# The last of 32 attention periods split into two of 256 queries, and three of four last output tiles finished from copied partial sums

## The chip, the cores and the metric

One NeuronCore of one Trainium2 chip runs the whole kernel. The metric is device time in microseconds (us) of one launch; lower is better. A separate profiled execution gives the trace.

## The reference, cut to what matters

Inputs are `x` (2048 tokens of 512 features), two sets of weights (A and B), and a gate vector. Branch A is full attention with 32 heads of width 16; branch B is a dilated local attention (8 keys per query, step 2); a gate mixes the two for each token.

```python
qkv = x @ wqkv                                   # A: H = 32, Dh = 16, S = 2048
scores = einsum("bhqd,bhkd->bhqk", q, k) * Dh ** -0.5
p = softmax(scores); a = (p @ v) @ wo            # per head, then one projection
b = local_attention(x)                           # 8 keys per query, own weights
out = g * a + (1 - g) * b                        # g = sigmoid((x * gate_w).sum(-1))
```

The exponentials of branch A are 32 heads of 2048 x 2048 numbers. They are most of the work.

## The kernel before, in words

**Periods and blocks.** Branch A is cut into 32 periods (L416): four chunks of 512 queries (`QW`, L32), and in each chunk eight groups of four heads. Within a period a *block* is one key tile of 128 keys for one head: 16 tiles times 4 heads is 64 blocks of 128 x 512 scores. The scores of a block are one matmul of 32 rows (the head's features padded to a strip) by 512 query columns; four heads sit in four row strips of the array and run beside each other. Probabilities times values is one matmul of 17 output rows (16 values and the softmax sum) into a column strip of an accumulator bank in PSUM (`pv_mm`, L1230).

**Two ways to an exponential.** Most blocks go to ScalarE (ACT): the scores of three or two blocks fill one of two PSUM rings (`rA` with three banks, `rB` with two), and one ACTIVATE makes the exponential of 1536 or 1024 columns (L1391 to L1406). The table `n_dve` (L20) says how many blocks of each period go to VectorE (DVE) instead, in groups of three (`d_set`, L1295): one operation per block turns scores into bit patterns (tile `dt_a` or `wkv`), three more per group add offsets to the three blocks at once (tile `pd_a`), and each of the four versions is multiplied with its own weighted values. A DVE group is thus six DVE operations and twelve value matmuls, and costs ScalarE nothing. From period `FLAT0` on (L34, L1341) the offset operation is written as one run of 1536 elements instead of six runs of 256. Before, the last four periods have 12, 15, 15 and 15 blocks on DVE.

**End of a period.** When a period's accumulator is complete, DVE transposes it (`po1`, L1428), takes the reciprocal of the sums, multiplies by reciprocal and gate (`po2`, `po2a`, `po2b`; on GpSimd except in the last two periods, L1432), and after every second period transposes the result into `oat` (`po3`, L1449). These are the inputs of the output projection.

**Output.** For each of 16 tiles of 128 tokens (loop at L1475), a PSUM bank collects four matmuls of branch B (`obt` times `bwo`) and four of branch A (`oat` times `woarr`); the bank is copied to SBUF and sent to DRAM by one transfer of 128 KB. For the last chunk the fourth `oat` matmul exists only after the last period. Before, its tiles are treated in two ways: tiles 2 and 3 have their first matmuls (nh = 3) evacuated early into unused memory (`fa_view`, L1471) and the last matmul goes to a ring bank, and DVE adds the two; tiles 0 and 1 keep their partial sums in two pinned PSUM banks, the last matmul adds to them, and ScalarE copies them out. So behind the last `po3` there are four matmuls, two DVE adds, two ScalarE copies and four transfers (three issued by SP, one by ScalarE).

**What sets the order.** All operations are put into one list with estimated durations, due times and dependences, and `list_schedule` (L180) writes out one fixed order for each engine; engines then run in that order. The planner also puts in filler matmuls of zeros (`zeros`, L1555) where it sees TensorE with too little to do. Three PSUM banks (`Banks(3)`, L407) are shared by accumulators, DVE scores, projections and fillers; two more rings take the scores for ScalarE.

Of the kernel before, what the change touches and what calls it, by code (L numbers as in the profile page):

```python
# [19 lines left out]
    n_dve=(3, 3, 6, 6, 9, 9, 12, 12) + (12,) * 21 + (15,) * 3,  # L20
# [13 lines left out]
FLAT0 = 29  # L34
# [89 lines left out]
SMD = 0.0  # L124
FIN, QB, KB, WO = 52.0, 0.0, 0.0, 26.0
# [181 lines left out]
def kernel(  # L307
# [108 lines left out]
    periods = [(c_, i) for c_ in range(NC) for i in range(NG)]  # L416
    NP = len(periods)
    n_dve = cfg["n_dve"]
# [3 lines left out]
    for pi in range(NP):  # L422
        first_unit.append(nu)
        n = n_dve[pi]
        assert n % NGR == 0 and n <= 4 * NTD
        taken = [(t, j) for t in vtiles for j in range(4)][:n]
        rest = [(t, j) for t in range(NT) for j in range(4) if (t, j) not in taken]
# [429 lines left out]
    def q_pair(pi, dl, rel):  # L857
# [35 lines left out]
        def get(e):  # L893
            def s():
                qt_tiles[pi + e] = work.tile([128, QW], BF16, name="qt", tag="qt", bufs=4)
                SP.dma_start(out=qt_tiles[pi + e][:], in_=_ap(q_scr[8 * (pi + e):8 * (pi + e) + 1, :], [[QW, 128], [1, QW]]))
            return s
# [10 lines left out]

    for pi in range(2, NP, 2):
        q_pair(pi, S0[pi] - QD, max(19.0, S0[pi - 2] - 2.0))  # L910


# [311 lines left out]
    for pi in range(NP):  # L1224
        for j in range(4):
            todo[(pi, j)] = NT + (NV - 1) * sum(1 for g in seq[pi][1] for x in g if x[1] == j)
# [3 lines left out]
    def pv_mm(pi, t, j, rhs, lhs):  # L1230
        c_, i = periods[pi]
        if pi not in acc_tiles:
            acc_tiles[pi] = misc_ps([128, QW], tag="acc")
# [14 lines left out]
    def pv_run(mine, tn):  # L1248
# [4 lines left out]
        def pv():  # L1253
            js = [j for j in range(4) if (pi, j) in first_pv and todo[(pi, j)] >= 1]
            j0 = st["op"].js[0]
            for _ in range(st["op"].filled):
                assert j0 in js
                mm(acc_tiles[pi][32 * j0:32 * j0 + 32, :], z32[:], z_bc, False, False, tile_position=(0, 32 * j0))
            for g_, s_, _, t, j in mine:
                pv_mm(pi, t, j, g_["p"][:, s_, :], vp_all[:, t])  # L1260
# [5 lines left out]
        o = op("pe", 0.0, pv, tn + 3.0, mode="c", js=js, full=-(-len(js) // 4), fill=not first,  # L1266
               deps=[g_["ex"] for g_ in gs] + [o_v[(4 * periods[pi][1] + j, t)] for _, _, _, t, j in mine]
# [27 lines left out]
    def d_set(pi, gi, t, j, qk_, tn):  # L1295
# [18 lines left out]
        def dq():  # L1314
            st["x"] = misc_ps([128, QW])
            mm(st["x"][:], kt_all[32 * j:32 * j + 32, i, t * 128:(t + 1) * 128], qt_tiles[pi][32 * j:32 * j + 32, :],
               True, True, tile_position=(32 * j, 0))
# [4 lines left out]
        deps = [o_q[pi], o_k[i][t // TPC], o_vd[(4 * i + j, t)]]  # L1322
# [10 lines left out]
        vs = [o_vd[(4 * i + j_, t_)] for t_, j_ in zip(g["ts"], g["js"])]  # L1333
# [14 lines left out]
        def pv(m, pb):  # L1348
            def s():
                for n1, (t_, j_) in enumerate(zip(g["ts"], g["js"])):  # L1350
                    pv_mm(pi, t_, j_, pb[:, n1, 0:QW], vd_all[:, m - 1, t_ - (NT - NTD)] if m else vp_all[:, t_])
# [30 lines left out]
    for k, us in enumerate(sets):  # L1382
# [18 lines left out]
        kd = [o_k[periods[pi][1]][t // TPC] for pi, t, j in us]  # L1401
# [17 lines left out]
    for pi, (c_, i) in enumerate(periods):  # L1419
# [3 lines left out]
        if i % 2 == 0:  # L1423
            ott_tok[pi // 2] = tok("ott", 1)
        ta, to = tok("accT", 1), ott_tok[pi // 2]
        E = S0[pi + 1]

        def po1(pi=pi, st=st):  # L1428
            st["a"] = work.tile([128, BPC, 32], FP32, name="accT", tag="accT", bufs=1)
            V.transpose(out=st["a"][:].rearrange("p b d -> p (b d)"), in_=acc_tiles[pi][:])  # L1430

        by_v = PO_V or pi >= NP - 2  # L1432
        E_ = V if by_v else G

        def po2(pi=pi, st=st):
            rden = work.tile([128, BPC], FP32, name="rden", tag="rden", bufs=2)
            V.reciprocal(out=rden[:], in_=st["a"][:, :, DH:DH + 1].rearrange("p b o -> p (b o)"))
            st["rd"] = rden

        def po2a(st=st, c_=c_, E_=E_):  # L1440
            E_.tensor_tensor(out=st["rd"][:], in0=st["rd"][:], in1=g_rw[:, c_ * BPC:(c_ + 1) * BPC], op=ALU.mult)

        def po2b(pi=pi, st=st, E_=E_):
            rden = st["rd"]
            rd_bc = _ap(rden[:], [list(rden[:].ap[0]), [1, BPC], [0, DH]])
            E_.tensor_tensor(out=ott2[:, 0, :, DH * (pi % 2):DH * (pi % 2 + 1)], in0=st["a"][:, :, 0:DH], in1=rd_bc,
                            op=ALU.mult)

        def po3(pi=pi, c_=c_, i=i):  # L1449
            if c_ not in oat_tiles:  # L1450
                oat_tiles[c_] = work.tile([128, NH, QW], BF16, name="oat", tag="oat", bufs=1)
            V.transpose(out=oat_tiles[c_][:, i // 2, :], in_=ott2[:, 0].rearrange("p b d -> p (b d)"))
        a = op("dve", 0.64, po1, E - PO1D, deps=o_pv[pi], alloc=[ta], use=[acc_tok[pi], acc_two[pi]])
        tr_ = tok("rden", 2)
        a = op("dve", 0.29, po2, E + 4.0, deps=[a], alloc=[tr_], use=[ta])
        al, us = [to] if i % 2 == 0 else [], [ta, tr_] + ([to] if i % 2 else [])
        if by_v:
            a = op("dve", 0.0, po2a, E + 4.0, deps=[a, o_gr], use=[tr_], parts=TT(BPC))
            a = op("dve", 0.0, po2b, E + 4.0, deps=[a], alloc=al, use=us, parts=TT(BPC * DH))
# [7 lines left out]
        prev = [o_oat[pi - 2]] if pi > 1 else []  # L1467
        o_oat[pi] = op("dve", 0.64, po3, E + 6.0, deps=[a, half] + prev, alloc=[oat_tok[c_]] if i == 1 else [],
                       use=[to] + ([oat_tok[c_]] if i > 1 else []))

    def fa_view(tt):  # L1471
        flat = kt_all[:, 0:NG - 1, :].rearrange("p g s -> p (g s)")
        return flat[:, tt * 2 * QW:(tt + 1) * 2 * QW].bitcast(FP32)

    for t in range(NT):  # L1475
# [3 lines left out]
        ng = NG - 2 if last else NG  # L1479
        nh = ng // 2  # L1480
        E = S0[NG * c_ + ng]
        dl = E + (4.0 + 4.0 * tt if last else 2.0 + 4.0 * tt)
        pin = last and tt < 2
        if pin:
            dl = S0[NP] - 1.0
# [13 lines left out]
        def ab_ev(st=st, tt=tt, last=last):  # L1499
            if last:  # L1500
# [6 lines left out]
        def dout(st=st, t=t):  # L1507
            SP.dma_start(out=out2d[t * 128:(t + 1) * 128, :], in_=st["o"][:, 0:D])
        tk = tok("misc", 2)
        a = None  # L1510
        for k0 in range(0, DC + nh, 2):
            nk = min(2, DC + nh - k0)
            a = op("pe", WAVE(nk), ab_part(k0), dl - 2.0 + 0.3 * k0, full=nk,
                   deps=[a] if k0 else [o_oat[NG * c_ + ng - 1], o_wo] + ([d_last[0]] + o_pv[NP - 1][:len(o_pv[NP - 1]) - (8, 0)[tt]] if pin else []) + o_obt[t:t + 1],
# [5 lines left out]
        elif pin:  # L1520
            tos = tok("osb", 2)

            def tail(st=st, c_=c_, tt=tt):
                mm_ct(st["pf"], oat_tiles[c_][:, NH - 1, tt * 128:(tt + 1) * 128], woarr[:, NH - 1, :], False, True)

            def t_ev(st=st):
                st["o"] = work.tile([128, D], BF16, name="osb", tag="osb", bufs=2)
                A.copy(out=st["o"][:, 0:D], in_=st["pf"][:])
            b = op("pe", 0.26, tail, S0[NP] + 60 + tt, deps=[o_oat[NP - 1], a], use=[tk, oat_tok[c_]])
            b = op("act", 0.6, t_ev, S0[NP] + 3 + tt, deps=[b, a], alloc=[tos], use=[tk])  # L1530

            def dout_a(st=st, t=t):
                A.dma_start(out=out2d[t * 128:(t + 1) * 128, :], in_=st["o"][:, 0:D])
            op(("sp", "act")[tt], 0.6, (dout, dout_a)[tt], S0[NP] + 4 + tt, deps=[b], use=[tos], lat=2.2)
        else:
            a = op("dve", 0.61, ab_ev, dl, deps=[a], use=[tk])
            tag = ("rB", "rA")[tt - 2]
            otag = "kvs"
            tk, tos = tok(tag, 2 if tag == "misc" else 1), tok(otag, 2)
            E2 = S0[NP] - 2.0  # L1540

            def tail(st=st, c_=c_, tt=tt, tag=tag):
                st["pt"] = misc_ps([128, D], tag=tag)
                mm_ct(st["pt"], oat_tiles[c_][:, NH - 1, tt * 128:(tt + 1) * 128], woarr[:, NH - 1, :], True, True)

            def t_ev(st=st, t=t, otag=otag):
                st["o"] = work.tile([128, D if otag == "osb" else 2 * D], BF16, name="osb", tag=otag, bufs=2)
                V.tensor_tensor(out=st["o"][:, 0:D], in0=st["pt"][:], in1=st["fa"], op=ALU.add)
            b = op("pe", 0.26, tail, E2 + tt, deps=[o_oat[NP - 1], a], alloc=[tk], use=[oat_tok[c_]])
            b = op("dve", 0.61, t_ev, E2 + 1 + tt, deps=[b, a], alloc=[tos], use=[tk])  # L1550
            def dout_a(st=st, t=t):
                A.dma_start(out=out2d[t * 128:(t + 1) * 128, :], in_=st["o"][:, 0:D])
            op("sp", 0.6, dout, E2 + 2 + tt, deps=[b], use=[tos], lat=2.2)
# [46 lines left out]
```

## Time and profile before

| what | us |
|---|---|
| three runs of the kernel | 805.14, 806.64, 807.27 |
| median | 806.64 |
| the profiled execution's own time | 805.02 |
| its span in the trace | 803.2 |
| ScalarE busy, share of the span | 778.0, 97% |
| TensorE busy (pipelined, not a measure of peak) | 742.8, 92% |
| VectorE busy | 689.1, 86% |
| GpSimd busy | 634.5, 79% |

Times in the trace count from the start of the span. A row of the timeline gives the start, the length, the engine, and how many instructions of one kind were merged into it; a bracket at the end gives idle time before it and what ended that. PE is TensorE, PEld its weight loads, ACT ScalarE, DVE VectorE, POOL GpSimd; SPq and ACTq are instructions that issue transfers. L378 and L369 are helpers that record every matmul and every instruction of the other engines, so operations are told apart by their tiles, not by their line.

### The profile page before, as it was taken

What the parts mean: (1) busy time and instruction counts of PE and PEld (TensorE: products, weight loads), DVE (VectorE), ACT (ScalarE), POOL (GpSimd) and SP (SyncE); (2) the same over time, 40 slices, a digit from 0 to 9 for tenths busy, and PEclk for the clock granted to TensorE, in tenths of its full rate; (3) what the DMA queues carried; (4) which work ended last, traced back from release to release, by engine and by line L of the source; (5) the groups of instructions that cost most, each with busy time, mean ns of one, the idle gap of its engine ahead of it and who ended that gap; (6) DMA issues with size and microseconds to landing.
All of it is one profiled execution on the core that took longest, in us unless ns stands there. A gap on an engine that the chain in (4) does not pass through costs nothing.

```text
span 803.2 us, 17445 instructions
## 1 busy us (share of the span) xinstructions
PE 742.8 (92%) x6651; PEld 240.5 (30%) x6708; DVE 689.1 (86%) x1098; ACT 778.0 (97%) x701; POOL 634.5 (79%) x1067
## 2 busy tenths in 40 slices
PE   8989999999999999999999999999989999889997
PEld 5333333332222222222222222222222323223222
DVE  5638787998896999999998999898998899888786
ACT  3999999999999999999999999999999999999996
POOL 4196979998999997999989899999999999940000
PEclk9999999999999999999999999999999999999999
DMA  8503171716345525245444535343534442000000
GB/s 264 145 16 106 30 168 53 170 42 165 86 93 138 126 74 151 60 117 122 110 108 116 123 98 139 82 118 108 142 85 105 128 119 62 19 8 21 1 1 28
DMA packets 58886, 77.19 MB, mean 96 GB/s; under 512 B 3745, under 2 KB 50849, under 8 KB 58801
## 3 DMA queue, kind: packets, MB, share of 16 engines
q1 hardware_dynamic: 52608, 53.91, 21.8%
q0 software_dynamic: 6048, 22.02, 14.7%
q8 instruction: 52, 0.85, 0.5%
q14 instruction: 34, 0.27, 0.1%
q10 hardware_dynamic: 144, 0.13, 0.0%
HBM read 43.78 MB, written 10.26 MB: 67 GB/s over the span
## 4 chain that ended last, share of the span: by engine, by line
ACT 50%; PE 25%; issue 22%; DVE 2%; DMA 1%; SPq 0%; ACTq 0%
ACT pT L369 49%; PE misc_ps L378 17%; PE ring L378 8%; DMA xld<-in_A_x_dram 1%; ACT lg L369 1%; DVE pd_a L369 0%; DVE wkv L369 0%; DVE kt_all L369 0%; PE pxt L635 0%; DVE dt_a L369 0%; DVE vd_all L369 0%; DVE vp_all L369 0%; ACT xT L369 0%; SPq L369 0%; DVE ssum L369 0%
## 5 line engine op out<-in xcount | busy, mean ns | idle before, releaser
L369 ACT ACTIVATE pT<-ring 128x1536 bf16<-128x1536 f32 (+1 forms) x677 | 769.5, 1324 | 8.8 <-PE ring L378 5.2
L378 PE MATMUL ring<-qt,kt_all 32*128 32x512 bf16 x1691 | 266.8, 382 | 45.5 <-ACT pT L369 37.2
L378 PE MATMUL misc_ps<-pT,vp_all 128*17 128x512 bf16 (+1 forms) x1691 | 201.6, 384 | 0.3 <-DVE dt_a L369 0.2
L369 POOL TENSOR_TENSOR prod<-ksh,qb 128x256 f32<-128x256 bf16 x256 | 174.4, 752 | 27.4 <-DMA ksh<-kv_scr 24.5
L378 PEld LDWEIGHTS <-kt_all 32*128 32x128 bf16 x2048 | 90.6, 91 | 297.8 <-issue 288.9
L369 POOL TENSOR_TENSOR prod<-prod 128x256 f32<-128x256 f32 (+1 forms) x256 | 172.0, 687 | 5.9
L369 DVE TENSOR_SCALAR pd_a<-wkv 128x1536 uint16<-128x1536 uint16 x198 | 169.1, 882 | 2.2 <-PE misc_ps L378 1.7
L369 DVE TENSOR_SCALAR wkv<-misc_ps 128x512 uint16<-128x512 f32 x198 | 132.3, 682 | 27.2 <-PE misc_ps L378 25.6
L369 DVE TENSOR_SCALAR pd_a<-dt_a 128x1536 uint16<-128x1536 uint16 x159 | 140.3, 905 | 0.9
L378 PE MATMUL misc_ps<-pd_a,vd_all 128*17 128x512 bf16 x1071 | 133.9, 382 | 0.1
L378 PE MATMUL misc_ps<-z 128*32 128x512 bf16 x399 | 132.3, 388 | 1.6 <-DVE z L369 1.6
L378 PE MATMUL misc_ps<-qt,kt_all 32*128 32x512 bf16 x357 | 129.0, 381 | 2.0 <-DVE wkv L369 0.5
L369 DVE TENSOR_SCALAR dt_a<-misc_ps 128x512 uint16<-128x512 f32 x159 | 106.6, 683 | 28.2 <-PE misc_ps L378 25.0
L369 POOL TENSOR_TENSOR prod<-vsh,lg 128x256 f32<-128x256 bf16 x128 | 82.7, 760 | 0.0
L378 PEld LDWEIGHTS <-vp_all 128*17 128x17 bf16 (+1 forms) x2048 | 54.3, 88 | 85.3 <-issue 72.5
L369 POOL TENSOR_TENSOR av<-vsh,lg 128x256 f32<-128x256 bf16 x128 | 77.7, 643 | 0.0
L378 PE MATMUL misc_ps<-bw,xT 128*128 128x512 bf16 x163 | 50.6, 384 | 1.9 <-issue 1.4
L378 PEld LDWEIGHTS <-vd_all 128*17 128x17 bf16 x1071 | 34.1, 88 | 51.7 <-issue 44.1
L378 PEld LDWEIGHTS <-z 128*32 128x32 bf16 x399 | 34.9, 96 | 44.8 <-issue 23.4
L369 POOL TENSOR_TENSOR rden<-rden,g_rw 128x16 f32<-128x16 f32 x30 | 8.8, 292 | 41.8 <-DVE rden L369 41.7
L378 PEld LDWEIGHTS <-xT 128*128 128x128 bf16 x576 | 28.7, 97 | 33.2 <-issue 30.2
L378 PE MATMUL misc_ps<-wkv,vp_all 128*17 128x512 bf16 x198 | 33.8, 384 | 0.0
(97 smaller groups left out, 531.2 us busy)
## 6 DMA issues: line engine op xcount, KB each, us to landing
ksh<-kv_scr SPq DMA_DIRECT2D x32, 512.0 KB
vsh<-kv_scr SPq DMA_DIRECT2D x32, 512.0 KB
av<-prod POOLq DMA_DIRECT2D x28, 512.0 KB, 6.7
av<-av POOLq DMA_DIRECT2D x14, 512.0 KB, 4.8
kv_scr<-kvs SPq DMA_DIRECT2D x16, 256.0 KB
qt<-q_scr SPq DMA_DIRECT2D x30, 128.0 KB
out_dram<-osb SPq DMA_DIRECT2D x15, 128.0 KB
xld<-in_A_x_dram SPq DMA_DIRECT2D x3, 512.0 KB
```

The lines of the kernel that those rows point to most:

```text
L369: return chain_on(key, f(*a, **k))
L378: return chain(nc.tensor.matmul(out, lhsT=lhsT, rhs=rhs, start=start, stop=stop, **kw))
```

## The change

The period list gets a 33rd entry: the last period's chunk and heads a second time. Its first half takes queries 0 to 255 of the last chunk, its second half queries 256 to 511. In these two half periods a block is **two** key tiles of one head, each against 256 queries, so a block is still 128 x 512 scores and fills the same ring slot; it needs two score matmuls of 256 columns in place of one of 512, and two value matmuls for each value matmul before. A half period has 32 such blocks. Both halves read the same query tile.

The blocks on DVE in the last five entries are 15, 15, 15, 6 and 6; before they were 12, 15, 15, 15 in four. `FLAT0` becomes 28, so the period that goes from 12 to 15 also uses the run of 1536.

The end of a period (`po1` to `po3`) works on 256 queries in the half periods, and on DVE in the last three entries, which are the same head groups as before. In the last chunk, output tiles 0, 1 and 3 now have their partial sums copied ahead by DVE, and only tile 2 keeps a pinned bank. Tiles 0 and 1 need only the first half period, so their last matmul, DVE add and transfer are due during the second half. Tiles 2 and 3 come after the second half: tile 2 through a ScalarE copy and a transfer issued by ScalarE, tile 3 through a DVE add and a transfer issued by SP. The pinned tile's matmuls wait for all but the last six value operations of the second half.

```diff
-    n_dve=(3, 3, 6, 6, 9, 9, 12, 12) + (12,) * 21 + (15,) * 3,
+    n_dve=(3, 3, 6, 6, 9, 9, 12, 12) + (12,) * 20 + (15,) + (15,) * 2 + (6, 6),
...
-FLAT0 = 29
+FLAT0 = 28
...
+    NQ = len(periods)
+    periods.append(periods[-1])
     NP = len(periods)
+    half_of = lambda pi: max(0, pi - NQ + 1) if pi >= NQ - 1 else None
+    tiles_of = lambda pi, t: [t] if half_of(pi) is None else [2 * t, 2 * t + 1]
+    q_cols = lambda pi: slice(0, QW) if half_of(pi) is None else slice(half_of(pi) * QW // 2, (half_of(pi) + 1) * QW // 2)
+    width = lambda pi: q_cols(pi).stop - q_cols(pi).start
+    parts_of = lambda pi, t: [(t_, slice(n_ * width(pi), (n_ + 1) * width(pi))) for n_, t_ in enumerate(tiles_of(pi, t))]
...
+    def pv_mm(pi, blocks, lhs):
+        for n_ in range(2):
+            for t, j, rhs in blocks:
+                for t_, cs in parts_of(pi, t)[n_:n_ + 1]:
+                    pv_one(pi, t_, j, rhs[:, cs], lhs(t_))
...
-            for s_, (pi, t, j) in enumerate(us):
-                mm(st["r"][:, s_, :], kt_all[32 * j:32 * j + 32, periods[pi][1], t * 128:(t + 1) * 128],
-                   qt_tiles[pi][32 * j:32 * j + 32, :], True, True, tile_position=(32 * j, 0))
+            for n_, s_ in [(n_, s_) for n_ in range(2) for s_ in range(len(us))]:
+                pi, t, j = us[s_]
+                for t_, cs in parts_of(pi, t)[n_:n_ + 1]:
+                    mm(st["r"][:, s_, cs], kt_all[32 * j:32 * j + 32, periods[pi][1], t_ * 128:(t_ + 1) * 128],
+                       qt_tiles[pi][32 * j:32 * j + 32, q_cols(pi)], True, True, tile_position=(32 * j, 0))
...
-        by_v = PO_V or pi >= NP - 2
+        by_v = PO_V or pi >= NP - 3
...
-        pin = last and tt < 2
-        if pin:
-            dl = S0[NP] - 1.0
+        pin = last and tt == 2
+        fa = last and tt != 2
...
-                   deps=[a] if k0 else [o_oat[NG * c_ + ng - 1], o_wo] + ([d_last[0]] + o_pv[NP - 1][:len(o_pv[NP - 1]) - (8, 0)[tt]] if pin else []) + o_obt[t:t + 1],
+                   deps=([a] if k0 else [o_oat[NQ - 3 if last else NG * c_ + NG - 1], o_wo]
+                         + ([d_last[0]] + o_pv[NP - 1][:n_pv - PIN0] if pin else [])) + o_obt[t:t + 1],
...
+        pe_ = S0[NQ] + 3.0 + 2.0 * tt if tt < 2 else S0[NP] + 60.0 + tt
...
+        b = op("pe", 0.22, tail, pe_, full=1, deps=[o_oat[NQ - 1 if tt < 2 else NP - 1], a], alloc=[] if pin else [tk2],
+               use=[oat_tok[c_]] + ([tk2] if pin else []))
+        b = op(*(("act", 0.6) if pin else ("dve", 0.61)), t_ev, pe_ + 1.5, deps=[b, a], alloc=[tos], use=[tk2])
+        op(*(("act", 0.6, dout_a) if pin else ("sp", 0.6, dout)), pe_ + 2.5, deps=[b], use=[tos], lat=2.2)
```

The score order of a set is: first halves of all its blocks, then second halves; value matmuls of a group are ordered in the same way (`pv_mm`).

More of the change, by code (lines that the diff above doesn't have):

```diff
@@ L425 @@
         assert n % NGR == 0 and n <= 4 * NTD
-        taken = [(t, j) for t in vtiles for j in range(4)][:n]
-        rest = [(t, j) for t in range(NT) for j in range(4) if (t, j) not in taken]
+        nt_ = NT // len(tiles_of(pi, 0))
+        vt_ = vtiles if nt_ == NT else [nt_ - 1, nt_ - 2]
+        taken = [(t, j) for t in vt_ for j in range(4)][:n]
+        rest = [(t, j) for t in range(nt_) for j in range(4) if (t, j) not in taken]
         own = []
@@ L1423 @@
         if i % 2 == 0:
[L1424 to L1425 removed]
+            ott_tok[c_, i // 2] = tok("ott", 1)
+        ta, to = tok("accT", 1), ott_tok[c_, i // 2]
         E = S0[pi + 1]
[L1428 to L1432 removed]
+        nb, b0 = width(pi) // 32, q_cols(pi).start // 32
@@ new lines, with tail @@
+            continue
+        if fa:
+            a = op("dve", 0.61, ab_ev, dl, deps=[a], use=[tk])
+        pe_ = S0[NQ] + 3.0 + 2.0 * tt if tt < 2 else S0[NP] + 60.0 + tt
+        tag = "rA" if tt == 3 else "misc"
+        tk2 = tk if pin else tok(tag, 1 if tag == "rA" else 2)
+        tos = tok("osb", 2)
+        def tail(st=st, c_=c_, tt=tt, pin=pin, tag=tag):
+            if not pin:
+                st["pf"] = misc_ps([128, D], tag=tag)
+            mm_ct(st["pf"], oat_tiles[c_][:, NH - 1, tt * 128:(tt + 1) * 128], woarr[:, NH - 1, :], not pin, True)
```

124 lines of the change are left out of this document (55 added, 69 removed).

## The prediction, made before the changed kernel ran

> **What bounds the kernel now.** I read the page first, then the busy times by stretch, then the timeline of the last 10 us, engine by engine.
>
> ```profile
> PE 742.8 (92%) x6651; PEld 240.5 (30%) x6708; DVE 689.1 (86%) x1098; ACT 778.0 (97%) x701; POOL 634.5 (79%) x1067
> ...
> L369 ACT ACTIVATE pT<-ring 128x1536 bf16<-128x1536 f32 (+1 forms) x677 | 769.5, 1324 | 8.8 <-PE ring L378 5.2
> ```
>
> ScalarE is busy for 97% of the span, nearly all of it in 677 exponentials, and sits idle only 8.8 us ahead of them. The next view shows the last three periods up to the last exponential, and the end.
>
> ```profile
> 726.00:794.50 68.50, 63.58 (x591) 19.40 (x594) 57.14 (x102) 68.42 (x61) 1.87 (x4) 1.00 0.02 7
> 794.50:803.20 8.70, 4.10 (x27) 1.50 (x19) 3.57 (x7) 1.09 (x3) 0.00 (x0) 0.91 0.19 62
> ```
>
> The columns after the length are PE, PEld, DVE, ACT and POOL, then the granted clock. From 726 to 794.5 ScalarE works 68.42 of 68.50 us, so there only fewer exponentials would help. From 794.5 it has 1.09 us of work left and the span still runs 8.7 us. That tail is a chain, which the timelines of ACT, PE, DVE and SP show:
>
> ```profile
> 738.24 56.28 ACT L369 ACTIVATE pT<-ring 128x1024 bf16<-128x1024 f32 x50
> 798.42 1.07 ACT L369 CAST osb<-misc_ps 128x512 bf16<-128x512 f32 x2 [3.90 <-PE misc_ps L378]
> 799.52 0.40 ACTq L369 DMA_DIRECT2D out_dram<-osb  x1
> ```
>
> ```profile
> 794.65 0.39 PE L378 MATMUL misc_ps<-pd_a,vd_all 128*17 128x512 bf16 x3
> ...
> 796.92 1.68 PE L378 MATMUL misc_ps<-woarr,oat 128*128 128x512 bf16 x7
> ```
>
> ```profile
> 795.09 0.72 DVE L369 STREAM_TRANSPOSE accT<-misc_ps 128x512 f32<-128x512 f32 x1 [1.37 <-PE misc_ps L378]
> 795.84 0.25 DVE L369 RECIPROCAL rden<-accT 128x16 f32<-128x16 f32 x1
> 796.13 0.17 DVE L369 TENSOR_TENSOR rden<-rden,g_rw 128x16 f32<-128x16 f32 x1
> 796.34 0.42 DVE L369 TENSOR_TENSOR ott<-accT,rden 128x256 bf16<-128x256 f32 x1
> 796.79 0.71 DVE L369 STREAM_TRANSPOSE oat<-ott 128x512 bf16<-128x512 bf16 x1
> 797.99 1.29 DVE L369 TENSOR_TENSOR osb<-misc_ps,kt_all 128x512 bf16<-128x512 f32 x2 [0.48 <-PE misc_ps L378]
> ```
>
> ```profile
> 798.71 1.31 SPq L369 DMA_DIRECT2D out_dram<-osb  x3
> ```
>
> The last exponential ends at 738.24 + 56.28 = 794.52, the last value matmul at 795.04, the `oat` transpose at 797.50. Then come four output matmuls, two adds and two copies, four transfer issues (SP's last ends at 800.02), and the span ends at 803.2.
>
> **The change, part by part.**
>
> *ScalarE's stream.* DVE takes 12 + 15 + 15 + 15 = 57 blocks before, 15 + 15 + 15 + 6 + 6 = 57 after. The order of ScalarE's instructions is the same in both kernels, the same 677 exponentials in the same widths, but for one CAST fewer at the end. So its 68.42 busy us stay, and time can be won only in the tail, or lost where a score set comes late.
>
> *The tail's DVE chain.* Five operations work on half as much. The two TENSOR_TENSOR rows above (16 elements 0.17, 256 elements 0.42) give (0.42 - 0.17) / 240 = 1.04 ns an element; no transpose of another width is in the trace, so I take that slope: accT 256 x 1.04 = 0.27, ott 128 x 1.04 = 0.13, oat 0.27, the gate product 0.01. For the reciprocal there are two widths:
>
> ```profile
> L369 DVE RECIPROCAL rden<-accT 128x16 f32<-128x16 f32 x32 | 7.8, 245 | 0.4
> L369 DVE RECIPROCAL rr<-ssum 128x32 f32<-128x32 f32 x16 | 5.6, 353 | 0.6
> ```
>
> That is 6.75 ns an element, 0.05 us for eight. Sum 0.73. If the transposes do not get shorter at all, 0.19; if all five halve, 1.13.
>
> *The last value matmuls.* Behind the last exponential the order now has four halves of two blocks and six of the last DVE group, in place of one and three whole ones. Rows for a half width are missing; those on either side are:
>
> ```profile
> 722.32 0.40 PE L1202 MATMUL misc_ps<-ident,obb 128*128 128x128 bf16 x4
> ...
> 791.07 0.39 PE L378 MATMUL ring<-qt,kt_all 32*128 32x512 bf16 x3
> 791.39 0.09 PEld L378 LDWEIGHTS <-vd_all 128*17 128x17 bf16 x3 [0.23 <-issue]
> 791.39 0.39 PE L378 MATMUL misc_ps<-pd_a,vd_all 128*17 128x512 bf16 x3
> 791.40 0.10 PEld L378 LDWEIGHTS <-vp_all 128*17 128x17 bf16 x4
> ```
>
> ```profile
> L1202 PE MATMUL misc_ps<-ident,obb 128*128 128x128 bf16 x64 | 6.3, 221 | 0.2 <-DVE dt_a L369 0.2
> ...
> L378 PE MATMUL misc_ps<-pd_a,vd_all 128*17 128x512 bf16 x1071 | 133.9, 382 | 0.1
> ```
>
> Four matmuls of 128 columns, each with its own weights, take 0.40: (0.40 - 0.22) / 3 = 0.06 from start to start. From 221 at 128 columns to 382 at 512 the length grows 0.42 ns a column, so 256 columns take 0.275 and follow each other after 0.108. The last half could then start 0.05 + 3 x 0.108 = 0.37 behind the exponential and end at 0.65, against 795.04 - 794.52 = 0.52 before. I take 0.05 lost, between nothing and 0.13.
>
> *The outputs.* Tiles 0 and 1 leave the tail. Before, SP's last issue begins about 0.44 (a third of 1.31) ahead of 800.02, 2.08 behind the transpose. After, two matmuls end at about 0.45 and 0.67 behind it; ScalarE copies (0.59) and issues at 1.1; DVE adds (0.69) and SP issues at 1.42. The transfers:
>
> ```profile
> 798.70:799.40 0.70, 0.00 (x0) 0.00 (x0) 0.58 (x1) 0.70 (x2) 0.00 (x0) 1.00 0.00 0
> 799.40:800.10 0.70, 0.00 (x0) 0.00 (x0) 0.00 (x0) 0.09 (x1) 0.00 (x0) 1.00 0.64 211
> 800.10:800.80 0.70, 0.00 (x0) 0.00 (x0) 0.00 (x0) 0.00 (x0) 0.00 (x0) 1.00 1.01 329
> 800.80:801.50 0.70, 0.00 (x0) 0.00 (x0) 0.00 (x0) 0.00 (x0) 0.00 (x0) 1.00 0.64 211
> ```
>
> The last column is GB/s. Traffic starts 0.7 behind the first issue (798.71), runs at up to 329 GB/s, where 128 KB (131,072 bytes) take 0.40, and is over at about 801.45; the span ends 1.75 later. With two tiles: 1.1 + 0.7 + 0.8 + 1.75 = 4.35 behind the transpose, against 803.2 - 797.5 = 5.7. That is 1.35 won; at least the 0.65 of the earlier issue, at most 1.4, if SP's transfer waits for nothing.
>
> *What moves into ScalarE's time.* The two adds (1.29 together) and two SP issues now run during the second half; SP has nothing else then. TensorE's two matmuls for them wait for the first half's `oat`, and behind them in TensorE's order stand six value halves and a score set, so ScalarE would wait next. Six score sets lie between the first half's last values and these matmuls: three pairs at 56.28 / 25 = 2.25, 6.8 us. DVE needs in that time its five shortened operations (1.55) and, by its order, four block and two offset operations:
>
> ```profile
> L369 DVE TENSOR_SCALAR wkv<-misc_ps 128x512 uint16<-128x512 f32 x30 | 20.1, 684 | 5.3 <-PE misc_ps L378 5.0
> L369 DVE TENSOR_SCALAR pd_a<-wkv 128x1536 uint16<-128x1536 uint16 x31 | 16.4, 564 | 1.0 <-PE misc_ps L378 0.9
> ```
>
> 4 x 0.68 + 2 x 0.56 = 3.86, together 5.4: 1.4 us of cover. If that is gone, each us late is a us lost. The third copy ahead (0.69) and the extra period end (1.55) are paid by three blocks fewer on DVE.
>
> *The halved passes.* At 0.108 two halves cost one whole, so TensorE's time stays; 156 more matmuls go in. [...]
>
> Sum: 0.73 - 0.05 + 1.35 = 2.0 us won, between 0.7 and 2.5. On the profiled execution's own 805.02 that gives 803.0. It was faster than all three runs, 1.6 below their median; on the median, **804.6**.
>
> **The rivals.**
>
> ```profile
> 706.00:709.50 3.50, 3.50 (x26) 0.74 (x23) 2.39 (x4) 2.99 (x3) 3.34 (x6) 0.52 0.00 0
> ```
>
> ```profile
> 708.17 1.02 ACT L369 ACTIVATE pT<-ring 128x1024 bf16<-128x1024 f32 x1 [0.21 <-PE misc_ps L378]
> 709.95 1.45 ACT L369 ACTIVATE pT<-ring 128x1536 bf16<-128x1536 f32 x1 [0.75 <-PE misc_ps L378]
> ```
>
> *The half clock goes.* At 706 the granted clock falls to 0.52 for 3.5 us, and ScalarE loses 0.21 + 0.75 = 0.96. The orders part here: 15 blocks put one more DVE score into the gap before it. Without the fall: 803.6. Against it: that score runs beside others and fills no time.
>
> *A half clock comes.* Matmuls of zeros fill TensorE's gaps, by the first row 15.5 us of 69.6 (the second row, TensorE's waits for a free ring, serves below):
>
> ```profile
> 725.00:794.60 69.60, 15.53 (x49) 4.35 (x48) 0.00 (x0) 1.00 0.03 7
> ```
>
> ```profile
> PE ring L378 <- ACT pT L369: 3.7, 8, 0.9
> ```
>
> Behind the point where the orders part the new one has 53 of them where the old had 61, and few in the first half period. If the clock falls there for one such stretch, about 1.0 is lost: 805.6. The clock at 1.00 over the 69.6 us speaks against it.
>
> *DVE late at the end.* The adds stand ahead of the last two offset operations. DVE was done 1.37 ahead of accT, at 793.72, 0.8 before the last exponential's end; 1.29 more leaves it 0.5 behind. Then 0.6 is given back: 805.2.
>
> *Weights of a second half wait for the first.* Each score set's second half loads weights into the strips that the first half is using. If they wait, 21 sets lose a load (0.10) each, 2.1 us if ScalarE feels all: 806.7. The rows at 791.39 and 791.40 show loads under running matmuls in column strips; for row strips no row decides. [...]
>
> *Halves drain the array (slower).* From scores at 791.07 to values at 791.39 is 0.32, against the 0.21 (512 x 0.42 ns) of passes of one kind: 0.11 of drain. If a second half drained and reloaded, 0.21 each, about 50 passes in the two halves (21 score sets, 13 value groups, 16 of DVE) cost 10.5; TensorE's waits in a third of the stretch (3.7 x 22 / 69.6 = 1.2) cover little. Net 9.3: 813.9. From (2.42 + 2.0 + 1.2) / 50 = 0.11 a pass the kernel is slower by over 0.3%. Against it: the 128-column row, where each matmul brings new weights and none drains.
>
> **How the numbers follow.** Forecast 52%; half clock gone 17%; half clock comes 12%; DVE late 8%; loads wait 5%; drain 6%. 0.3% of 806.64, about what a measurement of this kernel can tell, is 2.42. The clock's going passes it (2.0 + 0.96); of the forecast's own 52% four in ten, since its bounds reach 2.5 and three runs spread over 2.1: faster 0.17 + 0.21 = 0.38. Slower is the drain, 0.06. The rest is 0.56. The range runs from 802.6 (803.6 less half that spread) to 807.0, which takes in all but the drain and some strays.
>
> **What would show it.** ScalarE's last exponential still ends near 794.5; accT and oat near 0.45; two issues behind oat; 4.4 from oat's end to the span's. A starved ring between 772 and 795, or a clock under 1 there, would make it wrong. Loads that wait show as second score halves more than 0.11 behind the first.

## The result, and the profile after

| | before | after |
|---|---|---|
| median of 6 runs each, us | 806.25 (804.49 to 807.27) | 803.23 (802.41 to 803.60) |
| the profiled execution's own time | 805.02 | 803.36 |
| its span | 803.24 | 801.58 |

The ratio is 0.9967, 95% interval 0.9955 to 0.9979: faster by 0.33%, 3.0 us in the medians. The forecast was 804.6, range 802.6 to 807.0. The two profiled executions differ by 1.66 only, and both differences have to be explained.

The page of the kernel after, engine line:

```profile
PE 741.8 (93%) x6806; PEld 243.6 (30%) x6864; DVE 687.4 (86%) x1105; ACT 777.5 (97%) x700; POOL 638.2 (80%) x1067
```

155 more matmuls are in the trace, and TensorE is busy 1.0 us less, so the sum shows no added time for the halves (before's also holds its stretch at half clock). The busy times after, up to the last exponential's end and behind it (PE, PEld, DVE, ACT, POOL, clock):

```profile
726.00:794.88 68.88, 64.29 (x735) 23.21 (x737) 56.85 (x104) 68.73 (x62) 1.87 (x4) 1.00 0.03 10
794.88:801.58 6.70, 3.09 (x27) 1.05 (x27) 2.25 (x6) 0.59 (x2) 0.00 (x0) 1.00 0.12 40
```

ScalarE still idles only 0.15 us up to its last exponential, at 794.88. The tail is 6.70 instead of 8.72. Its timelines on DVE, TensorE, ScalarE and SP:

```profile
795.69 0.45 DVE L370 STREAM_TRANSPOSE accT<-misc_ps 128x256 f32<-128x256 f32 x1 [1.79 <-PE misc_ps L379]
796.17 0.20 DVE L370 RECIPROCAL rden<-accT 128x8 f32<-128x8 f32 x1
796.41 0.17 DVE L370 TENSOR_TENSOR rden<-rden,g_rw 128x8 f32<-128x8 f32 x1
796.62 0.29 DVE L370 TENSOR_TENSOR ott<-accT,rden 128x128 bf16<-128x128 f32 x1
796.94 0.45 DVE L370 STREAM_TRANSPOSE oat<-ott 128x256 bf16<-128x256 bf16 x1
798.09 0.69 DVE L370 TENSOR_TENSOR osb<-misc_ps,kt_all 128x512 bf16<-128x512 f32 x1 [0.70 <-PE misc_ps L379]
```

```profile
793.53 0.37 PE L379 MATMUL ring<-qt,kt_all 32*128 32x256 bf16 x2
794.06 0.81 PE L379 MATMUL misc_ps<-bwo,obt 128*128 128x512 bf16 x3 [0.16 <-issue]
794.80 0.40 PE L379 MATMUL misc_ps<-pT,vp_all 128*17 128x256 bf16 x8
...
795.25 0.38 PE L379 MATMUL misc_ps<-pd_a,vd_all 128*17 128x256 bf16 x2
795.57 0.82 PE L379 MATMUL misc_ps<-woarr,oat 128*128 128x512 bf16 x3
```

```profile
791.89 2.99 ACT L370 ACTIVATE pT<-ring 128x1536 bf16<-128x1536 f32 x3
797.87 0.59 ACT L370 CAST osb<-misc_ps 128x512 bf16<-128x512 f32 x1 [2.99 <-PE misc_ps L379]
798.49 0.37 ACTq L370 DMA_DIRECT2D out_dram<-osb  x1
```

```profile
798.81 0.33 SPq L370 DMA_DIRECT2D out_dram<-osb  x1
```

The last value matmul ends at 795.25 + 0.38 = 795.63, 0.75 behind the exponential (before 0.52). From accT's start to oat's end it is 1.70 (before 2.42). From oat's end, 797.39, to the end of the span it is 4.19 (before 5.73). ScalarE's issue comes 1.10 behind oat, SP's 1.42.

### The profile page after: what moved, and what is told of

The parts are those of the page before. It is cut to its first block, busy times and chain, and to the rows that moved or that the text cites. A ratio compares the mean times of both kernels' runs of the same rounds, so it can differ in the third digit from the quotient of the medians.

```text
span 801.6 us, 17762 instructions
## 1 busy us (share of the span) xinstructions
PE 741.8 (93%) x6806; PEld 243.6 (30%) x6864; DVE 687.4 (86%) x1105; ACT 777.5 (97%) x700; POOL 638.2 (80%) x1067
## 4 chain that ended last, share of the span: by engine, by line
ACT 49%; PE 25%; issue 21%; DVE 4%; DMA 1%; SPq 0%; ACTq 0%; DVEq 0%
ACT pT L370 48%; PE misc_ps L379 16%; PE ring L379 8%; DVE pd_a L370 1%; DMA xld<-in_A_x_dram 1%; DVE dt_a L370 1%; ACT lg L370 1%; DVE vd_all L370 1%; DVE wkv L370 0%; DVE kt_all L370 0%; PE pxt L645 0%; DVE vp_all L370 0%; DVE ssum L370 0%; DVE rr L370 0%; DVE qa L370 0%
## 5 line engine op out<-in xcount | busy, mean ns | idle before, releaser
L379 PE MATMUL ring<-qt,kt_all 32*128 32x512 bf16 (+1 forms) x1743 | 266.2, 375 | 44.3 <-ACT pT L370 36.4
L379 PE MATMUL misc_ps<-pT,vp_all 128*17 128x512 bf16 (+2 forms) x1743 | 202.7, 377 | 0.4 <-DVE dt_a L370 0.2
L370 POOL TENSOR_TENSOR prod<-ksh,qb 128x256 f32<-128x256 bf16 x256 | 177.7, 765 | 29.6 <-DMA ksh<-kv_scr 26.8
L370 DVE TENSOR_SCALAR pd_a<-wkv 128x1536 uint16<-128x1536 uint16 x198 | 166.1, 866 | 2.3 <-PE misc_ps L379 1.7
L379 PE MATMUL misc_ps<-pd_a,vd_all 128*17 128x512 bf16 (+1 forms) x1107 | 134.8, 375 | 0.2
L379 PE MATMUL misc_ps<-qt,kt_all 32*128 32x512 bf16 (+1 forms) x369 | 129.0, 373 | 3.4 <-DVE dt_a L370 1.8
L379 PE MATMUL misc_ps<-z 128*32 128x512 bf16 (+1 forms) x391 | 128.7, 386 | 1.6 <-DVE z L370 1.6
L379 PEld LDWEIGHTS <-vp_all 128*17 128x17 bf16 (+1 forms) x2112 | 56.1, 88 | 86.6 <-issue 74.2
L379 PEld LDWEIGHTS <-vd_all 128*17 128x17 bf16 x1107 | 36.0, 88 | 50.2 <-issue 41.8
L379 PE MATMUL misc_ps<-wkv,vp_all 128*17 128x512 bf16 (+1 forms) x207 | 33.0, 372 | 0.0
```

The source lines that it names most:

```text
L370: return chain_on(key, f(*a, **k))
L379: return chain(nc.tensor.matmul(out, lhsT=lhsT, rhs=rhs, start=start, stop=stop, **kw))
```

## The experiments

A fall of the clock is read in two ways: a profile gives the granted clock by the time, and each timed run gives its mean. A mean of 0.998 or less is counted as a run with a fall. The count is not sharp: half clock behind TensorE's last matmul slows no matmul and lowers the mean too (in e4's profile from 801.22 to the end, in before's 0.50 from 801.70 on, where the last matmul ended at 798.60), and before's lowest mean, 0.992, is by an estimate 0.008 x 808 / 0.50, some 13 us at half clock, so several falls of 3.41 us in one run. Times are medians of the runs; "before" is always the kernel before on the same chip in the same stretch of runs. "Tail" runs from the last exponential's end to the span's end, in the profiled execution. Tail intervals are taken from single starts and ends in the traces.

### How much of the difference lies between runs of one kernel: e1, e6

e1 is the kernel before, e6 the kernel after, both unchanged.

> The kernel before, unchanged, to see how often its clock falls. Theory (the change wins 2.0 us in the tail and nothing else; the half-clock stretch of 3.5 us at 706 in the profiled execution is chance): its executions differ in their mean clock, some 1.000, some 0.997 or 0.998, and those with the lower clock are about 1 us longer; median near 806.2. Rival (the order of the kernel before makes the clock fall every time and the new order never): every execution shows a mean clock of 0.998 or less.

Measured: 806.54, ratio to the other runs of before 0.9994 (0.9980 to 1.0008). 9 of 12 runs had a fall and a mean of 806.73; the other three 804.43. In the profile the fall is at 120 us, not at 706. So one kernel has falls in different places, and in some runs none: the rival that it is there every time has failed.

> The changed kernel once more, unchanged, with before on the same chip. Theory: two things make the 3.0 us. Runs at full clock are 2.0 to 2.4 below those of before (802.8 to 803.2), which is the tail; the rest is that a fall of the granted clock, 1.2 to 1.6 us each, comes in 60% of the runs of before and in 20 to 35% of these. Median 803.2. Rival: the falls are as common in both kernels, and six runs were luck; then 60% of the runs have a fall and the median is 804.2, 2.0 below before.

Measured: 802.51, five runs, ratio 0.9966 (0.9954 to 0.9978); one had a fall (803.50), four had not (mean 802.49). Together with the first six runs:

| | runs | with a fall | their mean | the others' mean |
|---|---|---|---|---|
| before, all runs of e1, e6 and e9 | 109 | 67 | 806.58 | 804.99 |
| after | 11 | 3 | 803.56 | 802.66 |

Without a fall the kernels differ by 2.33. Runs with falls are longer by 1.6 before and by 0.9 after. The rival (as many falls in both) gets no support, but eleven runs are few.

### What sets the falls off: e4, e8, e10, e11, e12

e4 is the kernel before with three matmuls of zeros ahead of one DVE score at 706:

```diff
             st["x"] = misc_ps([128, QW])
+            if pi == 28 and gi == 0 and n_ == 2:
+                for _ in range(3):
+                    mm(st["x"][0:32, :], z32[:], z_bc, True, True, tile_position=(0, 0))
```

> The kernel before with three more matmuls of zeros, ahead of the third DVE score of the period that starts near 704, in the place where TensorE sits idle for about 1 us just before the clock falls. Their results are overwritten by that score. Theory A (the idle gap is what lets the clock fall): no half-clock stretch near 706 in any execution, 1.0 us faster than the kernel before in its executions with a fall, the same as its others. Theory B (the fall depends on other things than this gap): clocks and times as in the kernel before, 806.2.

Measured: 805.16, ratio 0.9987 (0.9973 to 1.0002); 3 of 12 runs with a fall. Fewer, not none: the place at 120 was not filled.

What happens there starts on GpSimd. The timelines of POOL, DVE and ACT in the kernel after:

```profile
113.21 0.90 POOL L370 DMA_DIRECT2D av<-av  x1 [1.06 <-DMA av<-prod]
113.87 2.14 POOL L370 TENSOR_TENSOR prod<-prod 128x256 f32<-128x256 f32 x2
```

```profile
114.03 1.40 DVE L370 TENSOR_SCALAR kt_all<-kt_all,rowc,negk 128x2048 bf16<-128x2048 bf16 x1
115.35 2.37 DVE L370 TENSOR_TENSOR vd_all<-vp_all,wts 128x1632 bf16<-128x1632 bf16 x1
```

```profile
120.06 2.36 ACT L370 ACTIVATE pT<-ring 128x1536 bf16<-128x1536 f32 x2 [0.83 <-PE ring L379]
```

And of POOL, DVE, TensorE and ACT in e1:

```profile
113.40 0.90 POOL L369 DMA_DIRECT2D av<-av  x1 [1.25 <-DMA av<-prod]
```

```profile
114.04 1.59 DVE L369 TENSOR_SCALAR kt_all<-kt_all,rowc,negk 128x2048 bf16<-128x2048 bf16 x1
115.55 2.37 DVE L369 TENSOR_TENSOR vd_all<-vp_all,wts 128x1632 bf16<-128x1632 bf16 x1
```

```profile
118.58 0.37 PE L378 MATMUL misc_ps<-qt,kt_all 32*128 32x512 bf16 x1 [1.16 <-DVE dt_a L369]
```

```profile
120.25 2.37 ACT L369 ACTIVATE pT<-ring 128x1536 bf16<-128x1536 f32 x2 [1.02 <-PE ring L378]
122.92 2.37 ACT L369 ACTIVATE pT<-ring 128x1536 bf16<-128x1536 f32 x2 [0.30 <-PE ring L378]
125.82 1.45 ACT L369 ACTIVATE pT<-ring 128x1536 bf16<-128x1536 f32 x1 [0.53 <-PE ring L378]
```

GpSimd waits for a transfer; how long differs from run to run (idle 1.06 in after, 1.25 in e1, 3.32 in before). When it goes on, two long DVE operations run beside it and take longer than in before (kt_all 1.40 in after and 1.59 in e1 against 0.81, vd_all 2.37 in both against 1.85), a DVE score comes late, TensorE waits (1.16 in e1), and ScalarE loses 0.83 in after and 1.02 in e1. In before's first profile that transfer came 2.3 us later, when DVE was nearly through (POOL, DVE, ACT):

```profile
115.51 0.90 POOL L369 DMA_DIRECT2D av<-av  x1 [3.32 <-DMA av<-prod]
```

```profile
114.07 0.81 DVE L369 TENSOR_SCALAR kt_all<-kt_all,rowc,negk 128x2048 bf16<-128x2048 bf16 x1
114.79 1.85 DVE L369 TENSOR_TENSOR vd_all<-vp_all,wts 128x1632 bf16<-128x1632 bf16 x1
```

```profile
109.14 13.72 ACT L369 ACTIVATE pT<-ring 128x1024 bf16<-128x1024 f32 x12
```

There ScalarE runs through. The ten traces without zeros at this place agree: in eight GpSimd goes on at 113.1 to 113.6, kt_all takes 1.36 to 1.83 and ScalarE idles 0.81 to 1.51; in before and e6 it goes on at 115.5 and 116.8, kt_all takes 0.81 and ScalarE does not idle. No run moved that transfer to test it, and what stretches kt_all the traces do not show: in after it (114.03 to 115.43) lies beside the two prod operations (113.87 to 116.01), but in before a later kt_all of the same size (118.37), beside two other prod operations (117.98 to 119.72), takes 0.83.

In e1 the clock falls as well, and 1.02 - 0.83 + 0.30 + 0.53 = 1.0 more goes. When does it fall? In every trace the stretches at half clock ahead of the tail are 3.41 us long. In before the clock changes at 706.13, 709.54 and 801.70; the last two are 92.16 apart, 27.0 times 3.413, and the trace's record of the clock begins at 6.40, 205.0 times 3.413 ahead of 706.13. In after the record is one piece at full clock from 6.59 to 801.90, 233.0 times 3.413. Laid on a grid of that length, the stretch ahead of a fall and the fall, in before (706) and e1 (120):

```profile
702.72:706.13 3.41, 2.02 (x26) 0.65 (x26) 2.87 (x6) 3.41 (x4) 2.75 (x6) 1.00 0.01 2
706.13:709.54 3.41, 3.41 (x25) 0.69 (x23) 2.26 (x3) 2.86 (x3) 3.33 (x6) 0.50 0.00 0
```

```profile
116.94:120.35 3.41, 2.25 (x23) 0.83 (x23) 3.41 (x5) 2.39 (x4) 3.33 (x5) 1.00 0.14 26
120.35:123.76 3.41, 3.41 (x27) 1.10 (x25) 3.18 (x6) 3.11 (x3) 3.41 (x6) 0.50 0.00 0
```

And the grid in after, which has the same idle stretches and no fall:

```profile
115.82:119.23 3.41, 2.41 (x17) 0.64 (x17) 3.41 (x4) 3.41 (x4) 3.41 (x4) 1.00 0.43 80
702.91:706.32 3.41, 2.81 (x31) 0.89 (x29) 2.18 (x4) 3.41 (x4) 3.41 (x7) 1.00 0.01 2
706.32:709.73 3.41, 2.47 (x27) 0.73 (x26) 2.87 (x6) 3.41 (x4) 2.69 (x5) 1.00 0.00 0
```

TensorE's busy time ahead of a fall is 2.02 and 2.25, without one 2.41 and more. At these two places the six falls of all traces came behind 2.02 to 2.26; three stretches of 2.25 (e5, e9) and all of 2.31 and more had none. But busy time alone does not decide. At 549 to 550 TensorE has a gap of 0.95 as well, and in e3 a stretch as short as these has no fall behind it:

```profile
550.06:553.47 3.41, 2.11 (x24) 0.67 (x23) 3.25 (x6) 3.41 (x5) 3.41 (x7) 1.00 0.00 0
553.47:556.88 3.41, 3.41 (x36) 1.00 (x34) 3.41 (x5) 3.41 (x4) 3.32 (x6) 1.00 0.39 101
```

It is so in e4, e5, e9 and e10 too (2.05 to 2.09). What the limit is, the traces do not show. The grid's place differs from run to run (an edge at 706.13 in before, 706.32 in after, 707.51 in e7), so the same gap lies now in one stretch, now in two. The six falls came behind stretches with 1.15 to 1.39 us idle in all.

e8, e10, e11 and e12 fill both places. Four more zeros go ahead of the score that waits at 118, into the accumulator, where they need not wait (in e10 at 117.74, below, no idle time stands ahead of them):

```diff
+            if pi == 3 and gi == 1 and n_ == 1:
+                for _ in range(4):
+                    mm(acc_tiles[pi][0:32, :], z32[:], z_bc, False, False, tile_position=(0, 0))
             st["x"] = misc_ps([128, QW])
```

> The kernel of e7 with seven zero matmuls: four into the accumulator ahead of the DVE score that waits at 117.4 to 118.6 us, three ahead of a DVE score at 706. Theory: the falls at 120 and at 706 follow from those two idle stretches of TensorE (0.97 to 1.2 us); filled, they vanish: at most 1 run of 12 with a mean clock of 0.998 or less, all others within 0.6 us, median 802.5. Rival: the fall comes from elsewhere (power, or the other work on the chip): as large a share of falls as in e6 and e7.

> The changed kernel with the seven zero matmuls of e8 and nothing else. Theory: they take away the falls of the clock at 120 and 706; at most 1 or 2 of 12 runs show a mean clock of 0.998 or less. By the 803.58 of e8 (tail 6.85), time 803.4, so no gain over the changed kernel's own full-clock runs. Rival: as many falls as in e6 and e7 together (6 of 16).

> The kernel before with the same seven zero matmuls, so that the change is seen without the clock: e11 less e10. Theory: falls in at most 2 of 12 runs (before: 44 of 77), time 805.0 to 805.5, and e11 less e10 is the tail alone, 2.0 (8.75 less 6.70). Rival: the half periods also save or cost something ahead of the tail that a fall now and then hid: a difference under 1.6 or over 2.5.

> The changed kernel with PIN0 = 0 and the seven zero matmuls: what the runs so far point to as the best version. Theory: the tail of e9 (6.4) and no falls: 803.1, 0.3 below e10, all runs within 0.6. Rival: the tail gains nothing (see e9): 803.4, as e10.

| | time | ratio to before | runs with a fall | tail |
|---|---|---|---|---|
| e8: after, PIN0 = 16, zeros | 803.61 | 0.9974 (0.9962 to 0.9986) | 1 of 12 | 6.85 |
| e10: after, zeros | 803.39 | 0.9965 (0.9954 to 0.9977) | 1 of 12 | 6.69 |
| e11: before, zeros | 805.38 | 0.9997 (0.9985 to 1.0008) | 3 of 12 | 8.78 |
| e12: after, PIN0 = 0, zeros | 803.06 | 0.9966 (0.9953 to 0.9979) | 0 of 9 | 6.35 |

With both places filled the four have 5 falls in 45 runs. Kernel by kernel: after and its versions 2 in 33 with the zeros and 20 in 46 without (after, e3, e7, e9), before 3 in 12 (e11, one more than expected) and 67 in 109. In e12 the stretch around 118, now with the zeros:

```profile
115.74:119.16 3.42, 3.42 (x23) 1.04 (x22) 3.25 (x4) 3.42 (x4) 3.34 (x4) 1.00 0.34 65
```

So idle stretches at the two places cause most of the falls. Before with one place filled (e4) also has 3 in 12, so the share of each place is open, and no trace shows where the falls that are left lie. e11 less e10, the change with the falls out of the way, is 1.99; the tails differ by 8.78 - 6.69 = 2.09. e8's 802.5 was missed by 1.1: its PIN0 did not shorten the tail (see e7), and the zeros are not free. e10's runs without a fall have a mean of 803.43 against after's 802.66, e12's 803.07 against e9's 802.65. The traces show where: the four zeros also stand ahead of ScalarE's next scores, and in all four runs ScalarE idles 0.78 behind them, in e8, e10 and e11 with kt_all at its 0.80. On TensorE and ScalarE in e10:

```profile
117.74 1.04 PE L379 MATMUL misc_ps<-z 128*32 128x512 bf16 x4
```

```profile
120.41 2.37 ACT L370 ACTIVATE pT<-ring 128x1536 bf16<-128x1536 f32 x2 [0.78 <-PE ring L379]
```

The zeros thus win nothing in the median.

### What the earlier blocks on DVE do: e2

e2 is the kernel before with the extra three blocks earlier, and no half periods:

```diff
-    n_dve=(3, 3, 6, 6, 9, 9, 12, 12) + (12,) * 21 + (15,) * 3,
+    n_dve=(3, 3, 6, 6, 9, 9, 12, 12) + (12,) * 20 + (15,) * 3 + (12,),
-FLAT0 = 29
+FLAT0 = 28
```

> The kernel before with only the DVE blocks moved: 15, 15, 15, 12 in the last four periods in place of 12, 15, 15, 15, and the run of 1536 from the first of them on; nothing is halved. Theory (the gain beyond the tail is chance of the clock): the same as before, within 0.5 us, and a tail of 8.7 us from the last exponential's end. Rival (moving the blocks takes the clock's fall away): 1.0 us faster, about 805.2, with a mean clock of 1.000 in every execution.

Measured: 804.46, ratio 0.9979 (0.9965 to 0.9994); 3 of 12 runs with a fall. The time is 0.7 below what the rival had (805.2): a part of the gain needs no half periods. But falls had not gone. The runs without one have a mean of 804.23, 0.76 below before's, and the tail accounts for 0.64 of that. It was 8.08: value matmuls 0.43 behind the exponential, and 5.17 from oat to the end in place of 5.73, although the four issues come at the same 1.20, 1.63, 2.02 and 2.07 behind oat. That was expected by neither theory.

### Why the same four issues end 0.56 earlier: e5

The transfers of before at the end (797 to 805 us, 0.2 us a column), and of e5:

```profile
GB/s 0 0 0 0 0 0 0 0 0 0 0 0 56 343 246 251 328 338 328 323 328 77 20 26 41 0 0 0 0 0 0 0 0 0 0 0 0 0 0 0
...
q14 instruction: 2, 0.02, 0.8%
```

```profile
GB/s 0 0 0 0 0 0 0 0 0 0 0 0 0 0 0 0 0 0 87 389 180 287 338 307 379 384 266 5 0 0 41 0 0 0 0 0 0 0 0 0
...
q14 instruction: 1, 0.01, 0.3%
```

In before an 8 KB packet of instructions (0.54 us, 3.0 behind oat) comes among the output transfers, and a trickle of 77, 20 and 26 GB/s stays behind. It goes with DVE's count of instructions: in all four traces with before's DVE order (before, e1, e4, e11) it comes 3.0 behind oat, behind DVE's 1215th instruction (semaphores counted). In e2, whose order differs, it comes at 787.5, ahead of the tail. e5 puts 12 more instructions on DVE in period 10:

```diff
+    spare = const.tile([128, 32], BF16, name="spare")
         def p1():
+            if pi == 10:
+                V.memset(spare[:], 0.0)
             V.tensor_scalar(out=g["dt"][:, n_ * QW:(n_ + 1) * QW].bitcast(U16), in0=st["x"][:], ...
```

> The kernel before with 12 idle memsets of 32 columns on DVE in period 10, one ahead of each block's conversion. They cost DVE well under 1 us where it has 14% to spare. Theory: in the tail of before an 8 KB fetch of DVE's code lies among the last output transfers and delays one by 0.5; 12 more instructions move that fetch some 10 us ahead of the tail. The span then ends 5.2 us behind the oat transpose instead of 5.75, the tail is 8.1 to 8.2 instead of 8.7 to 8.8, and the runs at full clock have a mean near 804.7, 0.55 below 805.25. Rival: the third transfer is late because four tiles share the queues; then 5.75 and 805.25 stay.

Measured: the packet comes at 794.1, ahead of the tail (the one that is left, at 803.1, lies behind the output's traffic); 5.10 from oat to the end, tail 8.10: the theory holds in the trace. The time does not show it: 805.48, ratio 0.9999 (0.9991 to 1.0008), as 9 of 11 runs had a fall. Two had none (804.41, 804.59; before on that chip 804.83), too few to tell.

### What the two fewer tiles are worth: e3

e3 is the kernel after, but output tiles 0 and 1 wait for the second half period too:

```diff
-        pe_ = S0[NQ] + 3.0 + 2.0 * tt if tt < 2 else S0[NP] + 60.0 + tt
+        pe_ = S0[NP] + 60.0 + (tt + 2 if tt < 2 else tt - 2)
...
-        b = op("pe", 0.22, tail, pe_, full=1, deps=[o_oat[NQ - 1 if tt < 2 else NP - 1], a], alloc=[] if pin else [tk2],
+        b = op("pe", 0.22, tail, pe_, full=1, deps=[o_oat[NP - 1], a], alloc=[] if pin else [tk2],
```

(and the two tiles use other SBUF buffers).

> The changed kernel, but output tiles 0 and 1 wait for the second half's transpose too, so that four output matmuls, three DVE adds, one ScalarE copy and four transfers stand behind it. Theory (two thirds of the tail's gain is the outputs that left it): 1.2 us slower than the changed kernel, about 804.4, with 5.4 us from the end of the last oat transpose to the end of the span in place of 4.2, and the chain from accT to oat still 1.7. Rival (the transfers' fixed time hides the number of tiles): 803.2, as the changed kernel.

Measured: 804.66, ratio 0.9976 (0.9962 to 0.9990), 8 of 12 runs with a fall. DVE's timeline at its end:

```profile
797.94 0.45 DVE L370 STREAM_TRANSPOSE oat<-ott 128x256 bf16<-128x256 bf16 x1
799.08 1.89 DVE L370 TENSOR_TENSOR osb<-misc_ps,kt_all 128x512 bf16<-128x512 f32 x3 [0.70 <-PE misc_ps L379]
```

Three adds, the last issue 2.62 behind oat, and 5.31 from oat to the end: 1.12 more than after, and within 0.1 of what was expected. The value matmuls ended 0.43 behind the exponential; here two of the pinned tile's matmuls were ahead of the last score set.

### Why the last values are late: e7, e9

Both are the kernel after with one number changed, how many of the last value operations the pinned tile's matmuls need not wait for:

```diff
-PIN0, PIND, FA0, FA1 = 6, 7.0, 4.0, 4.0
+PIN0, PIND, FA0, FA1 = 16, 7.0, 4.0, 4.0   # e7; e9: 0, 7.0, 4.0, 4.0
```

> The changed kernel with PIN0 = 16: TensorE's order then has the last six DVE value halves and eight value halves ahead of the pinned tile's first four matmuls, and only four value halves behind the last exponential. Theory: the four matmuls of the pinned tile are why the last value matmul ends 0.75 behind the last exponential; now 0.45 to 0.5, the rest of the tail as it was, so the tail is 6.4 instead of 6.70 and the runs at full clock 0.25 below those of the changed kernel. Rival: the halved value matmuls need that time by themselves: 0.65 or more stays, and the tail stays at 6.6 to 6.7.

Measured: 803.60, ratio 0.9982 (0.9973 to 0.9991), 5 of 11 runs with a fall; the value matmuls end 0.91 behind the exponential, tail 6.84. Both expectations missed it. Its order has eight value halves ahead, but then two bwo matmuls still stand between them and the last four halves, now right under the last exponential's end.

> The changed kernel with PIN0 = 0: the pinned tile's four bwo matmuls wait for all value matmuls, so TensorE's order has only four value halves behind the last exponential and the seven matmuls of the pinned tile behind those. In e7 two of the four matmuls were still ahead of them, and the last value matmul ended 0.91 behind the last exponential. Theory: matmuls of the pinned tile ahead of the last value halves are the reason in both; now 0.43 to 0.5, and the seven (1.5) run beside DVE's chain (1.7). Tail 6.35 to 6.45 instead of 6.70; runs at full clock 0.25 to 0.3 below the changed kernel's 802.5 to 802.8, so 802.3 to 802.5. Rival: the seven matmuls then end behind oat and give it back: oat to the end of the span 4.4 to 4.7 instead of 4.2, tail 6.7.

```profile
795.35 0.38 PE L379 MATMUL misc_ps<-pT,vp_all 128*17 128x256 bf16 x3
795.66 1.04 PE L379 MATMUL misc_ps<-bwo,obt 128*128 128x512 bf16 x4
796.53 0.81 PE L379 MATMUL misc_ps<-woarr,oat 128*128 128x512 bf16 x3
797.51 0.60 PE L379 MATMUL misc_ps<-woarr,oat 128*128 128x512 bf16 x2 [0.17 <-DVE oat L370]
```

Measured: value matmuls end at 795.73, 0.43 behind the exponential (795.30), the seven matmuls end ahead of oat, tail 6.35: the theory holds. Time 802.99, ratio 0.9965 (0.9953 to 0.9976), 4 of 12 runs with a fall, the others' mean 802.65, where 802.3 to 802.5 was expected. That is not measurably better than after (802.66). With the falls out of the way (e12 against e10) it is 0.33 better, as the tails say. No version beats after clearly.

## Why the prediction was right, point by point

**ScalarE's stream.** Right. The orders are the same up to 706. From the 601st exponential's start to the 677th's it is 86.27 in after, 86.16 to 86.17 in e1, e4 and e11, which have no fall there. The 0.11 is not the price of the half periods: e2, with the blocks moved and nothing halved, has 86.26. In the profile of before the fall makes it 87.33.

**DVE's chain.** 0.73 forecast, 0.72 measured (2.42 to 1.70); both transposes took 0.45, as forecast from the slope.

**The last value matmuls.** The step that was too small: 0.05 forecast, between nothing and 0.13; measured 0.75 - 0.52 = 0.23. I counted only the value halves behind the exponential. TensorE's order also has the pinned tile's four bwo matmuls (three are recorded, 794.06 to 794.87) behind the last score set, so eight halves that were ready wait behind them. e9 moved them and got 0.43; the six DVE halves come earlier there too, so that is the worth of both.

**The outputs.** The term that was too small the other way: 1.35 forecast, within 0.65 to 1.4; measured 5.73 - 4.19 = 1.54. The issues came at 1.10 and 1.42, exactly as worked out. Two fewer tiles are worth 0.9 to 1.0 (5.10 to 5.17 in e5 and e2, to 4.19); the other 0.56 to 0.63 is the packet of instructions, which I had read into the price of four tiles. In after it lies at 793.4, ahead of the tail. That is luck of the instruction count.

**The sum.** 2.0 forecast, 2.02 in the tail, as the two errors cancel, which is luck too: without the packet in before's tail it would have been 1.4 to 1.5. e11 less e10 gives 1.99 in time.

**Why the medians differ by 3.0.** Faster by over 0.3%, as it came out, had a chance of 0.38, a result within 0.3% one of 0.56; the tail's 2.0 alone would have stayed within. Runs without a fall differ by 2.33, and before has more falls: (67/109) x 1.6 - (3/11) x 0.9 = 0.74 on the mean. This is the rival *the half clock goes*, which stood at 17% and 0.96: half right. The fall does not go for good. It comes in some runs of after as well (e6: at 706, behind the same 2.02 us of busy TensorE as in before, so the added score filled no time, as argued), in others of before not at all. Whether the change itself makes it rarer is open: e3, e7 and e9, variants of after, had 17 falls in 35 runs. Of the 2.33 the tail explains 2.0; the rest was not settled. With the zeros in both (e11, e10) the runs without a fall differ by 1.92, and no rest shows.

**Why the profiles differ by 1.66 only.** The last exponential ended 0.36 later. Up to the 601st exponential after loses 1.35: 0.83 at 119, where GpSimd's transfer came early, and 0.45 at 573, where a DVE operation (qa) had taken 1.41 in place of 0.33. From there before loses 1.06, in its fall; after loses 0.07 in the last exponential. That part has nothing to do with the change, and the forecast from one profile could not see it.

**Weights that wait, halves that drain.** Both rivals fell. One score set of three blocks in halves, on TensorE's timeline of after:

```profile
789.01 0.40 PE L379 MATMUL ring<-qt,kt_all 32*128 32x256 bf16 x6 [0.94 <-ACT pT L370]
```

Six halves take 0.40, one takes 0.26 to 0.28: the second halves start 0.11 to 0.12 behind the first, each with weights of its own in a strip that is in use. That is the edge of the sign given (more than 0.11), but ScalarE's stream lost at most 0.11 in all, not 2.1. **A half clock comes** did not happen: it is 1.00 from 726 on. **DVE late** did not come: it was done 1.79 ahead of accT.

## What to carry to other kernels

Halve the last unit of work, so that what must follow the last result is shorter (here 1.70 us from accT to oat in place of 2.42) and the other half's outputs leave beside it; count all that an engine's order puts between the last producer and the end, not only what belongs to the unit. Before a gain of 0.3% is put down to an edit, look at whether the runs differ in something that the edit doesn't touch, such as the granted clock, and make both kernels equal in it (e11 against e10). Where a profiled execution has a stall, ask first whether it is there in the next execution.

## What the runs showed of the hardware

- Half-clock stretches ahead of the tail were 3.41 us long, at a granted clock of 0.50, on a grid whose place differs by run (an edge at 706.13 in before, 706.32 in after, 707.51 in e7). The six in the traces followed stretches with TensorE busy for 2.02 to 2.26 us of 3.41; five others of 2.05 to 2.12 had none behind them, so busy time alone does not foretell a fall. Runs with falls were longer by 0.9 us (after) and 1.6 us (before).
- A packet of 8 KB of instructions (0.54 us, in before at 800.50) among the last output transfers put the end off by 0.56 to 0.63; 12 more instructions on DVE moved it ahead of the tail (e5, 794.1).
- DVE's kt_all operation took 0.81 alone and, in eight traces, 1.36 to 1.83 beside GpSimd's first prod operations behind that wait (0.83 in before at 118.37, beside later ones); which one it was went with the end of GpSimd's wait for a transfer (113.1 to 113.6, or 115.5 and later). ScalarE idled 0.81 to 1.51 in those eight and not at all in the other two.
- Matmuls of 256 columns, each with new weights, followed each other after 0.11 in row and in column strips.
